# An mLSTM cell and a squared-ReLU feed-forward in one kernel: q C in twos, and another order of work in the first eight chunks

## The chip, the core and the metric

The kernel runs on one core of a Trainium2 chip. The metric is the device time of one execution in microseconds; the kernel before takes 527.05 us, the median of three runs (526.32 to 527.27). The core's engines are TensorE (PE in the profile, with its weight loads as PEld), VectorE (DVE), ScalarE (ACT), GpSimd (POOL) and the queues that start DMA transfers (SP). Each engine works through its own instructions in the order of the program and waits for the others by semaphores. The order within an engine is therefore part of the program, and a wait of one instruction holds up everything behind it on that engine.

## The reference, cut to what matters

Attention part: 4 batches, 8 heads, 768 steps, head size 40. A matrix memory C and a vector n are carried along the steps:

```python
for t in range(S):
    m_new  = np.maximum(f_gate[:, :, t] + m, i_gate[:, :, t])
    f_stab = np.exp(f_gate[:, :, t] + m - m_new)
    i_stab = np.exp(i_gate[:, :, t] - m_new)
    m = m_new
    C = f_stab * C + i_stab * outer(v_t, k_t)
    n = f_stab * n + i_stab * k_t
    h_tilde = C @ q_t
    denom = np.maximum(np.abs(n . q_t), 1.0)
    y[:, :, t] = sigmoid(o_gate_t) * h_tilde / denom
```

The result, taken as 3072 rows of 320 numbers, goes through the feed-forward part (w_in 320 x 2048, w_out 2048 x 320):

```python
h = np.maximum(x @ w_in, 0.0)
return h * h @ w_out
```

The weights arrive as 64-bit floats, that is as pairs of 32-bit words, and the kernel makes 32-bit floats of them itself ("rounding").

## The kernel before

The steps are cut into 24 chunks of 128. For each chunk TensorE turns k and q (chunks 0 to 6), forms the scores k q, and multiplies the weighted scores P with v, and, where the chunk is not the first of its batch, q with the memory C of the chunks before. VectorE weights the scores (`weighted`), normalises the result to x, squares the feed-forward's hidden values (`square_half`) and does most of the rounding. ScalarE makes the decay weights W, the relu and copies out of PSUM. Two chunks make a group of 256 rows for the feed-forward: `ffn1` (x w_in, in four steps a group) and `ffn2` (times w_out).

From chunk 6 on the attention works on turned tiles: q C and v P give num with the head's columns in the partitions. This is the kernel before, with P=128, H=8, PR=4, DP=64, D=40, D1=41:

```python
def attend_turned(s):
    ...
    halves = [slice(DP * i, DP * (i + 1)) for i in range(2)]
    live = [slice(DP * i, DP * i + D) for i in range(2)]
    numT = [ps_at.tile([P, W], F32, name="numT", tag="at")[:].rearrange("p (c t) -> p c t", t=P) for _ in range(2)]

    if c > 0:                                            # q C
        C = C_b[(s - 1) % 2]
        for e in range(2):
            for i, g in ((0, 0), (1, 1), (0, 1), (1, 0)):
                j = 2 * e + g
                nc.tensor.matmul(                        # L508
                    numT[i][halves[g], e, :], lhsT=C[live[i], j * D1 : j * D1 + DP], rhs=d["eA"][live[i], j, :],
                    start=(e == 0), stop=False, skip_group_check=True,
                )
    for i in range(2):                                   # v P
        for e in range(2):
            for g in range(2):
                ...
                nc.tensor.matmul(                        # L517
                    numT[i][halves[g], e, :], lhsT=va_w[s % NKQ][:, h * D1 : h * D1 + DP], rhs=..., ...)
    ...                                                  # dC (L527), then a DVE transpose of each numT (L534)
```

Rounding of one piece of the weights: two instructions on ScalarE (`words`), three on VectorE and an addition on GpSimd (`join`). A `step` does the words of the next piece ahead and joins one piece:

```python
def words(self):
    ...
    nc.scalar.activation(mag[:, :w], raw[:, :, 1].bitcast(F32), AF.Abs)                                   # L195
    nc.scalar.activation(low[:, :w], raw[:, :, 0].bitcast(U32), AF.Copy, bias=2.0, scale=2.0 ** -51)      # L197
def join(self):
    nc.vector.tensor_scalar(mag, mag, ...)                                     # L206
    nc.vector.tensor_scalar(bits, bits, scalar1=3, ..., op0=ALU.logical_shift_left)   # L210
    nc.vector.scalar_tensor_tensor(bits, in0=self.raws[n][:, :w, 1], ...)      # L211
    nc.gpsimd.tensor_tensor(dst.bitcast(I32), bits, low.bitcast(I32), op=ALU.add)     # L215
    self.fetch()
def step(self):
    if len(self.b) < len(pieces):
        if len(self.a) == len(self.b):
            self.words()
        self.words()
        self.join()
```

The start and the loop over chunks 2 to 5. `idle(n)` lets TensorE multiply n times with zeros; `weigh(s + 1)` masks on GpSimd (L358) and makes W on ScalarE (L382); P is made on VectorE (L433):

```python
idle(12)
transposes(0)                # four turns of k, then four of q, and their copies
idle(4)
scores(0)
idle(3)
...
for u in range(8):
    s = 2 + u // 2
    relu_half()                                  # ACT, L660
    if u % 2 == 0:
        if u == 0:
            ffn1(0, 0)
            scores(s)
            rounding.step()
        else:
            turn_rows(s - 1)                     # turns x on TensorE, L618
            scores(s)
            ffn1(u // 4, u % 4)
        ...
        weighted(s)
        if u == 2:
            ...
        else:
            weigh(s + 1)
            square_half()
    else:
        ...
        attend(s)                                # q C (L442), dC (L449), P v (L456)
        if u == 3:
            square_half()
        rounding.join()
        normalise(s)                             # L578 to L588, makes x
        ...
        transposes(s + 1)
        rounding.words()
        ffn1(u // 4, u % 4)
        square_half()
    ...
    while rounding.done < NEXT[u]:
        rounding.step()
```

ffn1 takes its PSUM tiles from a pool of three (`ps_h`) and uses two a step, so its second tile waits for a relu of the step before. The scores, dC, q C and num take theirs from another pool of three (`ps_at`).

The loop over the later parts; chunk s = 6 + n // 4. The pieces of weights end in its first five passes:

```python
LAST = (21, 23, 25, 25, 26)
for n, (which, g, i) in enumerate(parts):
    s, at = 6 + n // 4, n % 4
    ...
    if at == 0:
        do(score, s)                             # scores and weighted
    if at == 1:
        do(attend_turned, s)
        ...
    if which == 1:
        ...                                      # ffn1
            for half in both:
                st["half"] = half
                relu_half()
                square_half()
    elif g == 0:
        ffn2(g, *divmod(i, 2))
    else:
        ffn2_fast(g, i)
    ...
    if n < 5:
        while rounding.done < LAST[n]:
            rounding.step()
```

Of the kernel before, what the change touches and what calls it, by code (L numbers as in the profile page):

```python
# [29 lines left out]
def kernel(  # L30
# [85 lines left out]
    def make_consts():  # L116
        for t in kq_b:
            nc.vector.memset(t[:, :, :, D:], 0.0)
        for t in va_b:
            nc.vector.memset(t[:, :, D:], 1.0)  # L120
        for t in va_w:
            nc.gpsimd.memset(t[:, H * D1 :], 0.0)
        nc.vector.memset(keep[:], 1.0)
        nc.vector.memset(keep[:, :, 0:1], 0.0)
        make_identity(nc, ident[:])

        nc.gpsimd.memset(sel[:], 0.0)
        nc.gpsimd.affine_select(
            sel[:], sel[:], compare_op=ALU.not_equal, fill=1.0, base=0, pattern=[[-1, H], [0, P]], channel_multiplier=1,
        )  # L130

        nc.gpsimd.memset(later[:], 0.0)
        nc.gpsimd.affine_select(
            later[:], later[:], compare_op=ALU.is_ge, fill=-1e30, base=0, pattern=[[1, P]], channel_multiplier=-1,
        )

        nc.gpsimd.memset(bdm[:], 1.0)
        nc.gpsimd.memset(bdm[:DP, :, 1, :], 0.0)
        nc.gpsimd.memset(bdm[DP:, :, 0, :], 0.0)


    def in_words(ap):
# [20 lines left out]
    class Rounding:  # L163
# [56 lines left out]
        def done(self):  # L220
            return len(self.b)

        def step(self):
            if len(self.b) < len(pieces):
                if len(self.a) == len(self.b):
                    self.words()
                self.words()
                self.join()

    rounding = Rounding()  # L230
# [168 lines left out]
        t = ps_o.tile([P, W], F32, name="tp", tag="o_ps") if o else ps_at.tile([P, W], F32, name="tp", tag="at")  # L399
        return t[:].rearrange("p (j t) -> p j t", j=PR)  # L400

    def transposes(s, o=(False, False)):
        d = st[s]
        kqT(s)
        for i, n in enumerate(("kT", "qT")):
            tp = bank(o[i])
            for j in range(PR):
                nc.tensor.transpose(  # L408
                    tp[:, j, :], d["kq"][:, i, 2 * j : 2 * j + 2, :].rearrange("p h d -> p (h d)"), ident[:],
                )  # L410
            (nc.scalar.copy if i == 0 or s in (0, *range(2, 7)) else nc.vector.tensor_copy)(d[n], tp)
# [78 lines left out]

    def attend_turned(s):

        b, c = divmod(s, NB)
        d = st[s]
        halves = [slice(DP * i, DP * (i + 1)) for i in range(2)]
        live = [slice(DP * i, DP * i + D) for i in range(2)]  # L500
        numT = [ps_at.tile([P, W], F32, name="numT", tag="at")[:].rearrange("p (c t) -> p c t", t=P) for _ in range(2)]

        if c > 0:
            C = C_b[(s - 1) % 2]
            for e in range(2):
                for i, g in ((0, 0), (1, 1), (0, 1), (1, 0)):
                    j = 2 * e + g
                    nc.tensor.matmul(  # L508
                        numT[i][halves[g], e, :], lhsT=C[live[i], j * D1 : j * D1 + DP], rhs=d["eA"][live[i], j, :],
                        start=(e == 0), stop=False, skip_group_check=True,  # L510
                    )
        for i in range(2):
            for e in range(2):
                for g in range(2):
                    j = 2 * e + g
                    h = PR * i + j
                    nc.tensor.matmul(  # L517
                        numT[i][halves[g], e, :], lhsT=va_w[s % NKQ][:, h * D1 : h * D1 + DP],
                        rhs=d["P"][h % 2][:, h // 2, :] if s < KQ_SQ else d["P"][i][:, j, :],
                        start=(c == 0 and e == 0), stop=True, skip_group_check=True,  # L520
                    )
        if c + 1 < NB:
            dC = ps_at.tile([P, PR, D1], F32, name="dC", tag="at")
            for j in range(PR):
                for i in range(2):
                    h = PR * i + j
                    nc.tensor.matmul(  # L527
                        dC[live[i], j, :], lhsT=d["kq"][:, 0, h, :D], rhs=d["vw"][:, h, :], start=True, stop=True,
                    )

        tn = attn.tile([P, P // SQ, PR, SQ], F32, name="tn", bufs=1)
        to = tn[:].rearrange("p m c r -> p c m r")
        for i in range(2):
            nc.vector.transpose(to[:, 2 * i : 2 * i + 2], numT[i][:, :2, :].rearrange("p c t -> p (c t)"))  # L534
        d["tn"] = tn
        if c + 1 < NB:
            Cn = C_b[s % 2][:, : PR * D1].rearrange("p (j d) -> p j d", d=D1)
            for rows in live:
                if c > 0:
                    nc.vector.tensor_tensor(Cn[rows], dC[rows], d["Cd"][rows], op=ALU.add)  # L540
                else:
                    nc.vector.tensor_copy(Cn[rows], dC[rows])
# [13 lines left out]
    def normalise_turned(s):  # L556
        d = st[s]
        N = d["N"].rearrange("p (g e j r) -> p g e j r", g=2, e=2, r=SQ)
        R = D - SQ
        den = N[:, :, 1, :, R]  # L560
        dm = work.tile([P, H], F32, name="dm")
        dm2 = dm[:].rearrange("p (j g) -> p g j", g=2)
# [5 lines left out]
        x4, og = x[:, :DM].rearrange("p (j g d) -> p g j d", g=2, d=D), d["og"].rearrange("p (j g) d -> p g j d", g=2)  # L568
# [242 lines left out]
    load_part(1, 2)  # L811
    fetch(1)
    idle(12)
    transposes(0)
    idle(4)
    scores(0)
    idle(3)
# [49 lines left out]
            if u == 0:  # L867
                ffn1(0, 0)
                scores(s)
                rounding.step()  # L870
            else:
                turn_rows(s - 1)
                scores(s)
                ffn1(u // 4, u % 4)
            if u == 2:
                rounding.words()
            weighted(s)
            if u == 2:
# [31 lines left out]
        if u < 4:  # L910
            load_o(4 + u)
        while rounding.done < NEXT[u]:
            rounding.step()
# [23 lines left out]
    for n, (which, g, i) in enumerate(parts):  # L937
# [41 lines left out]
        if which == 1:  # L979
# [3 lines left out]
            else:  # L983
# [55 lines left out]
```

## Time and profile before

| | |
|---|---|
| time, median of 3 | 527.05 us (526.32 to 527.27) |
| span of the profiled execution | 525.2 us |
| mean granted clock of TensorE | 0.994 |
| L508, q C of the turned chunks | 240 records, 10.4 us busy |
| L517, v P of the turned chunks | 288 records, 19.7 us busy |
| L534, transposes of num on VectorE | 36, mean 447 ns |
| DMA | 68.06 MB, mean 130 GB/s |

The busy time in 40 equal slices of 13.1 us (a digit is tenths; the last three rows are not engines: granted clock of TensorE, busy share of the DMA engines):

```
PE   9989989998999999999999999999999999999997
PEld 4868878885798898898898898898898898998997
DVE  8588988968864764655754755665755755522541
ACT  3767577552541431522432623322623413102000
POOL 3355633231210210110210200110201210000000
PEclk9997999999999999999999999999999999999999
DMA  9989699777586586586586576676556262110000
```

The busy time of TensorE counts overlapping instructions once. The ends of matmuls are modelled, so how long a block of matmuls takes is better read from the start of its first instruction to the start of the next block. A line of the profile names the source line, the engine, the operation, what is written and read, the shape, the count, and in brackets the idle time before it with what ended it.

### The profile page before, as it was taken

What the parts mean: (1) busy time and instruction counts of PE and PEld (TensorE: products, weight loads), DVE (VectorE), ACT (ScalarE), POOL (GpSimd) and SP (SyncE); (2) the same over time, 40 slices, a digit from 0 to 9 for tenths busy, and PEclk for the clock granted to TensorE, in tenths of its full rate; (3) what the DMA queues carried; (4) which work ended last, traced back from release to release, by engine and by line L of the source; (5) the groups of instructions that cost most, each with busy time, mean ns of one, the idle gap of its engine ahead of it and who ended that gap; (6) DMA issues with size and microseconds to landing.
All of it is one profiled execution on the core that took longest, in us unless ns stands there. A gap on an engine that the chain in (4) does not pass through costs nothing.

```text
span 525.2 us, 10338 instructions
## 1 busy us (share of the span) xinstructions
PE 515.1 (98%) x3929; PEld 449.8 (86%) x3929; DVE 331.8 (63%) x638; ACT 194.2 (37%) x460; POOL 88.2 (17%) x110
## 2 busy tenths in 40 slices
PE   9989989998999999999999999999999999999997
PEld 4868878885798898898898898898898898998997
DVE  8588988968864764655754755665755755522541
ACT  3767577552541431522432623322623413102000
POOL 3355633231210210110210200110201210000000
PEclk9997999999999999999999999999999999999999
DMA  9989699777586586586586576676556262110000
GB/s 193 225 207 194 158 161 202 190 184 155 117 162 121 126 173 126 124 168 127 135 162 132 122 151 125 149 158 135 133 122 128 69 130 43 61 36 2 26 25 26
DMA packets 239394, 68.06 MB, mean 130 GB/s; under 512 B 185744, under 2 KB 233872, under 8 KB 239344
## 3 DMA queue, kind: packets, MB, share of 16 engines
q1 hardware_dynamic: 239248, 67.20, 60.5%
q8 instruction: 31, 0.51, 0.4%
q10 hardware_dynamic: 96, 0.20, 0.1%
q14 instruction: 19, 0.16, 0.1%
HBM read 55.08 MB, written 17.86 MB: 139 GB/s over the span
## 4 chain that ended last, share of the span: by engine, by line
PE 87%; DVE 5%; ACT 3%; DMA 2%; SPq 2%; issue 1%; POOL 0%; ACTq 0%; DVEq 0%; POOLq 0%
PE h_ps L728 33%; PE h_ps L634 27%; PE h_ps L645 7%; PE tp L420 4%; PE numT L517 3%; PE h_ps L674 2%; PE hp L456 2%; PE numT L508 2%; PE idle L787 1%; DVE g L667 1%; PE tp L408 1%; SPq L308 1%; DMA num_rows<-tn 1%; PE A_ps L349 1%; PE dC L527 1%
## 5 line engine op out<-in xcount | busy, mean ns | idle before, releaser
L634 PE MATMUL h_ps<-xT,w_in 128*128 128x256 f32 x768 | 175.7, 384 | 0.6 <-ACT xT L619 0.6
L634 PEld LDWEIGHTS h_ps<-xT,w_in 128*128 128x128 f32 x768 | 144.2, 191 | 22.0 <-issue 1.2
L667 DVE TENSOR_TENSOR g<-r_sb 128x512 f32<-128x512 f32 x96 | 61.7, 702 | 66.5 <-ACT r_sb L660 66.5
L660 ACT ACTIVATE r_sb<-h_ps 128x512 f32<-128x512 f32 x96 | 49.9, 600 | 108.6 <-PE h_ps L645 105.5
L728 PE MATMUL h_ps<-w_out,g 128*128 128x160 f32 x528 | 77.0, 302 | 0.0
L728 PEld LDWEIGHTS h_ps<-w_out,g 128*128 128x128 f32 x528 | 72.5, 190 | 1.4
L358 POOL TENSOR_SCALAR_AFFINE_SELECT A_bc<-A_bc 128x1024 f32<-128x1024 f32 x22 | 24.3, 1103 | 214.2 <-ACT kq L368 155.4
L382 ACT ACTIVATE W_sb<-A_bc,b_T 128x128 f32<-128x128 f32 x176 | 53.8, 390 | 13.3 <-POOL A_bc L358 13.1
L728 PE MATMUL h_ps<-T,S 128*128 128x160 f32 x352 | 52.3, 302 | 0.0
L728 PEld LDWEIGHTS h_ps<-T,S 128*128 128x128 f32 x352 | 48.8, 190 | 3.0 <-ACT r_sb L660 3.0
L368 ACT ACTIVATE kq<-A_bc 64x512 f32<-64x512 f32 x30 | 18.9, 629 | 84.3 <-DMA A_bc<-a_rows 84.2
L645 PE MATMUL h_ps<-xT,w_in 64*128 64x256 f32 x384 | 49.0, 391 | 0.0
L645 PEld LDWEIGHTS h_ps<-xT,w_in 64*128 64x128 f32 x384 | 34.8, 186 | 12.3 <-issue 9.0
L744 DVE TENSOR_TENSOR y_sb<-y_sb,h_ps 128x160 f32<-128x160 f32 x44 | 14.1, 320 | 29.3 <-PE h_ps L728 28.7
L433 DVE TENSOR_TENSOR P_sb<-tp,W_sb 128x512 f32<-128x512 f32 x46 | 29.5, 684 | 3.6 <-PE tp L420 3.1
L534 DVE STREAM_TRANSPOSE tn<-numT 128x256 f32<-128x256 f32 x36 | 15.7, 447 | 23.2 <-PE numT L517 23.2
L394 POOL TENSOR_TENSOR vw<-va,W_sb 128x328 f32<-128x328 f32 x20 | 18.1, 904 | 66.0 <-ACT W_sb L382 60.3
L748 ACT COPY y_sb<-h_ps 128x160 f32<-128x160 f32 x11 | 3.2, 293 | 66.3 <-PE h_ps L728 66.3
L420 PEld LDWEIGHTS tp<-kqT 40*128 40x128 f32 x384 | 24.2, 187 | 3.3 <-issue 2.3
L420 PE MATMUL tp<-kqT 40*128 40x128 f32 x384 | 26.9, 279 | 0.0
L728 PE MATMUL h_ps<-T,g 128*128 128x160 f32 x176 | 25.7, 299 | 0.0
L728 PE MATMUL h_ps<-w_out,S 128*128 128x160 f32 x176 | 25.7, 299 | 0.0
(119 smaller groups left out, 592.0 us busy)
## 6 DMA issues: line engine op xcount, KB each, us to landing
A_bc<-a_rows SPq DMA_DIRECT2D x23, 512.0 KB, 4.7
raw<-in_moe_w_out_dram SPq DMA_DIRECT2D x16, 320.0 KB, 3.5
num_rows<-tn SPq DMA_DIRECT2D x18, 256.0 KB, 3.1
kq<-num_rows SPq DMA_DIRECT2D x72, 64.0 KB, 2.2
kqT<-kq_rows SPq DMA_DIRECT2D x34, 128.0 KB, 3.2
raw<-in_moe_w_in_dram SPq DMA_DIRECT2D x8, 512.0 KB, 5.2
kq<-in_k_dram SPq DMA_DIRECT2D x24, 160.0 KB, 4.7
va<-in_v_dram SPq DMA_DIRECT2D x24, 160.0 KB, 4.9
```

The lines of the kernel that those rows point to most:

```text
L358: nc.gpsimd.affine_select(A[:], A[:], compare_op=ALU.is_ge, fill=-1e30, base=0, pattern=[[0, H], [1, P]], channel_multiplier=-1,)
L368: nc.scalar.activation(e[rows], st[s]["A"][0][rows, PR * i : PR * (i + 1), :], AF.Exp)
L382: nc.scalar.activation(d["W"][:, i * n + h, :], A[i][:, h, :], AF.Exp, bias=b_T[:, b, c, i * n + h : i * n + h + 1],)
L394: nc.gpsimd.tensor_tensor(d["vw"][:], d["va"][:], d["W"][:, :, P - 1 : P].to_broadcast([P, H, D1]), op=ALU.mult,)
L420: nc.tensor.matmul(sc[i][:, j, :], lhsT=d["kT"][rows, j, :], rhs=d["qT"][rows, j, :], start=True, stop=True,)
L433: nc.vector.tensor_tensor(t, d["sc"][i], d["W"][:, heads, :], op=ALU.mult)
L517: nc.tensor.matmul(numT[i][halves[g], e, :], lhsT=va_w[s % NKQ][:, h * D1 : h * D1 + DP], rhs=d["P"][h % 2][:, h // 2, :] if s < KQ_SQ els ...
L634: nc.tensor.matmul(hs[i][:, n, :], lhsT=w_in[:, a, fb * P : (fb + 1) * P], rhs=xT[:, :, a, :], start=(n == 0 and a == 0), stop=False,)
L645: nc.tensor.matmul(hs[i][:, n, :], lhsT=w_in2[rows, 2 * pp + n, :], rhs=xT[rows, :, 2, :], start=False, stop=(n == 1),)
L660: nc.scalar.activation(rs[-1][:], h[:], AF.Relu)
L667: nc.vector.tensor_tensor(g4[:, :, i, :], r[:], r[:], op=ALU.mult)
L728: nc.tensor.matmul(to, lhsT=lhsT[:, p], rhs=rhs[:, p, :], start=(start and p == 0), stop=(p == NPAIR - 1), skip_group_check=True,)
```

## The change

The kernel after differs in these places.

- q C of the turned chunks: one num tile in one PSUM bank in place of two; pairs of matmuls (rows 0 to 39 of C into partitions 0 to 63, rows 64 to 103 into partitions 64 to 127) in place of groups of four over all row and column halves. v P follows the same order, one VectorE transpose takes the place of two, and normalisation reads the heads in the new order.
- First chunk: four multiplications with zeros between the turns of k and those of q, so that TensorE goes on working there. The zeroing of the ends of the v tiles on GpSimd comes later among the constants.
- Chunk 2: P is made ahead of the rounding step, so that TensorE need not wait for it behind that.
- Chunk 3: normalisation comes ahead of a rounding.
- Last pieces of weights: the words of the last piece are no longer made ahead, and the squares of pass 3 come after chunk 7's P in pass 4, so that P waits neither for the last transfer of weights nor for the squares.

```diff
-        for t in va_w:
-            nc.gpsimd.memset(t[:, H * D1 :], 0.0)
 ...
+        for t in va_w:
+            nc.gpsimd.memset(t[:, H * D1 :], 0.0)
 ...
-        def step(self):
+        def step(self, ahead=True):
             if len(self.b) < len(pieces):
                 if len(self.a) == len(self.b):
                     self.words()
-                self.words()
+                if ahead:
+                    self.words()
                 self.join()
 ...
-    def transposes(s, o=(False, False)):
+    def transposes(s, o=(False, False), apart=0):
 ...
         for i, n in enumerate(("kT", "qT")):
+            if i > 0 and apart:
+                idle(apart)
             tp = bank(o[i])
 ...
-        numT = [ps_at.tile([P, W], F32, name="numT", tag="at")[:].rearrange("p (c t) -> p c t", t=P) for _ in range(2)]
+        numT = ps_at.tile([P, PR, P], F32, name="numT", tag="at")
 ...
-            for e in range(2):
-                for i, g in ((0, 0), (1, 1), (0, 1), (1, 0)):
-                    j = 2 * e + g
+            for j in range(PR):
+                for i in range(2):
                     nc.tensor.matmul(
-                        numT[i][halves[g], e, :], lhsT=C[live[i], j * D1 : j * D1 + DP], rhs=d["eA"][live[i], j, :],
-                        start=(e == 0), stop=False, skip_group_check=True,
+                        numT[halves[i], j, :], lhsT=C[live[i], j * D1 : j * D1 + DP], rhs=d["eA"][live[i], j, :],
+                        start=(j == 0), stop=False, skip_group_check=True,
                     )
 ...  (v P in the same order)
-        for i in range(2):
-            nc.vector.transpose(to[:, 2 * i : 2 * i + 2], numT[i][:, :2, :].rearrange("p c t -> p (c t)"))
+        nc.vector.transpose(tn[:].rearrange("p m j r -> p j m r"), numT[:].rearrange("p j t -> p (j t)"))
 ...  (the order of heads in normalise_turned)
-    transposes(0)
+    transposes(0, apart=4)
 ...
             if u == 0:
                 ffn1(0, 0)
                 scores(s)
+                weighted(s)
                 rounding.step()
 ...
-            weighted(s)
+            if u > 0:
+                weighted(s)
 ...
             if u == 3:
                 square_half()
-            rounding.join()
-            normalise(s)
+                normalise(s)
+                rounding.join()
+            else:
+                rounding.join()
+                normalise(s)
 ...
         if at == 0:
             do(score, s)
+            if n == 4:
+                square_half()
+                square_half()
 ...
                     relu_half()
-                    square_half()
+                    if n != 3:
+                        square_half()
 ...
-                rounding.step()
+                rounding.step(ahead=rounding.done + 1 < LAST[2])
```

More of the change, by code (lines that the diff above doesn't have):

```diff
@@ L500, in attend_turned @@
         live = [slice(DP * i, DP * i + D) for i in range(2)]
-        numT = [ps_at.tile([P, W], F32, name="numT", tag="at")[:].rearrange("p (c t) -> p c t", t=P) for _ in range(2)]
+        numT = ps_at.tile([P, PR, P], F32, name="numT", tag="at")
         if c > 0:
             C = C_b[(s - 1) % 2]
-            for e in range(2):
-                for i, g in ((0, 0), (1, 1), (0, 1), (1, 0)):
-                    j = 2 * e + g
+            for j in range(PR):
+                for i in range(2):
                     nc.tensor.matmul(
-                        numT[i][halves[g], e, :], lhsT=C[live[i], j * D1 : j * D1 + DP], rhs=d["eA"][live[i], j, :],
-                        start=(e == 0), stop=False, skip_group_check=True,
-                    )
-        for i in range(2):
[L513 to L521, printed above, removed]
+                        numT[halves[i], j, :], lhsT=C[live[i], j * D1 : j * D1 + DP], rhs=d["eA"][live[i], j, :],
+                        start=(j == 0), stop=False, skip_group_check=True,
+                    )
+        for j in range(PR):
+            for i in range(2):
+                h = PR * i + j
+                nc.tensor.matmul(
+                    numT[halves[i], j, :], lhsT=va_w[s % NKQ][:, h * D1 : h * D1 + DP],
+                    rhs=d["P"][h % 2][:, h // 2, :] if s < KQ_SQ else d["P"][i][:, j, :],
+                    start=(c == 0 and j == 0), stop=True, skip_group_check=True,
+                )
         if c + 1 < NB:
@@ L531, in attend_turned @@
         tn = attn.tile([P, P // SQ, PR, SQ], F32, name="tn", bufs=1)
-        to = tn[:].rearrange("p m c r -> p c m r")
-        for i in range(2):
-            nc.vector.transpose(to[:, 2 * i : 2 * i + 2], numT[i][:, :2, :].rearrange("p c t -> p (c t)"))
+        nc.vector.transpose(tn[:].rearrange("p m j r -> p j m r"), numT[:].rearrange("p j t -> p (j t)"))
         d["tn"] = tn
@@ L561, in normalise_turned @@
         dm = work.tile([P, H], F32, name="dm")
-        dm2 = dm[:].rearrange("p (j g) -> p g j", g=2)
+        dm2 = dm[:].rearrange("p (g j) -> p g j", g=2)
         nc.vector.tensor_scalar(dm2, den, scalar1=-1.0, scalar2=1.0, op0=ALU.mult, op1=ALU.max)
@@ L567, in normalise_turned @@
         x3 = x[:, :DM].rearrange("p (h d) -> p h d", d=D)
-        x4, og = x[:, :DM].rearrange("p (j g d) -> p g j d", g=2, d=D), d["og"].rearrange("p (j g) d -> p g j d", g=2)
+        x4, og = x[:, :DM].rearrange("p (g j d) -> p g j d", g=2, d=D), d["og"].rearrange("p (g j) d -> p g j d", g=2)
         nc.vector.tensor_tensor(x4[:, :, :, :SQ], N[:, :, 0], og[:, :, :, :SQ], op=ALU.mult)
```

## The prediction

> **What bounds the kernel now.** I read the busy times first, then the list of waits of TensorE, then the single instructions of the stages that the diff touches.
>
> ```profile
> PE 515.1 (98%) x3929; PEld 449.8 (86%) x3929; DVE 331.8 (63%) x638; ACT 194.2 (37%) x460; POOL 88.2 (17%) x110
> ```
> TensorE (PE) is busy for 515.1 of 525.2 us. So the end moves for two reasons only: TensorE work is added or removed, or one of its few waits goes. Those waits, by what was waited for (total, times, longest):
>
> ```profile
> PE numT L508 <- DVE P_sb L433: 2.6, 1, 2.6
> PE tp L618 <- DVE x_sb L587: 1.7, 1, 1.7
> PE dC L449 <- DVE P_sb L433: 1.1, 1, 1.1
> PE h_ps L634 <- ACT xT L619: 0.6, 1, 0.6
> ```
> By start time they lie at 127.7, 68.2, 39.5 and 31.7 us; from 128 us to the end TensorE has no gap. Three are the targets of the diff: the last words and squares (127.7), chunk 3's normalisation (68.2), P of chunk 2 (39.5). After the last one, stretches of the span (length, then busy time and count for PE, PE loads, DVE, ACT, POOL, then TensorE's granted clock) show a second loss:
>
> ```profile
> 37.50:40.95 3.45, 2.37 (x22) 2.25 (x21) 3.08 (x6) 0.25 (x1) 2.29 (x3) 1.00 0.68 151
> 40.95:44.40 3.45, 3.45 (x19) 3.45 (x19) 2.54 (x6) 3.17 (x11) 0.89 (x2) 0.50 1.04 283
> 44.40:47.80 3.40, 3.40 (x11) 2.86 (x11) 3.30 (x5) 3.35 (x7) 3.16 (x4) 0.51 1.42 159
> ```
> Clock 0.50 for 6.8 us right after the wait: some 3.4 us of TensorE time.
>
> The part that the change undoes stands in each turned chunk. TensorE in order of time (start, length):
>
> ```profile
> 148.39 0.67 PE L508 MATMUL numT<-kq,C 40*64 40x128 f32 x16
> 148.99 1.09 PE L517 MATMUL numT<-P_sb,va 128*64 128x128 f32 x16
> 149.91 0.48 PE L527 MATMUL dC<-vw,kq 128*40 128x41 f32 x16
> ```
> q C (L508) and v P (L517) each have 16 records, two for each of 8 matmuls with 128 columns, but from start to start q C takes 0.60 us and v P 0.92. The single records show why: q C starts in fours, at 148.55, 148.66, 148.77 (109 ns apart); v P in twos, also 109 ns apart.
>
> [...] four q C records within 20 ns, and 172 ns without a weight load before q C and before v P. [...] The new q C pairs take different rows and different halves of one bank, [...] only v P's pairs (one bank, two halves, 109 ns) come near that, no trace has exactly the new form. [...] The trace shows the halving after 1.08 us of idling among small matmuls, but none after 1.75 and 2.6 us, [...]. [...] the shift L210 takes 0.43 us alone and 1.40 beside GpSimd.
>
> **The change part by part.**
>
> 1. q C in twos. Eight matmuls of two records: 4 groups of four x 109 ns = 436 ns become 8 pairs x 109 = 872 ns. [...] L508 has 240 records, 240 / 16 = 15 chunks. TensorE has no slack after 128 us, so all of it counts: 15 x 0.436 = **+6.5 us**. One VectorE transpose of 512 columns in place of two of 256 (0.45 us each), one PSUM bank less, and another order of heads: all off the path.
>
> 2. Last words and squares. ScalarE and VectorE around the wait of 127.7:
>
> ```profile
> 123.04 0.50 ACT L195 ACTIVATE mag<-raw 128x320 f32<-128x320 f32 x1 [5.75 <-DMA raw<-in_moe_w_out_dram]
> 123.84 2.04 ACT L660 ACTIVATE r_sb<-h_ps 128x512 f32<-128x512 f32 x4
> 124.44 2.50 DVE L667 TENSOR_TENSOR g<-r_sb 128x512 f32<-128x512 f32 x4 [1.64 <-ACT r_sb L660]
> 126.97 1.29 DVE L433 TENSOR_TENSOR P_sb<-tp,W_sb 128x512 f32<-128x512 f32 x2
> ```
> The last weight words wait for a DMA, the relus stand behind the words, the squares behind the relus, chunk 7's P behind the squares. Afterwards P comes right after the rounding at 122.8 and ends near 124.1; the q C of chunk 7 starts near 124.7 less the 1.2 gained earlier (below) and takes about 1.0, so v P, the first to need P, is due near 124.5. The q C of chunk 7 lasts from 124.69 to 128.38 = 3.69 us instead of 0.60: **-3.1 us**. The last rounded piece of w_out then lands near 128.6; the product needs it only near 130, so no new wait.
>
> 3. Chunk 3's normalisation. VectorE ends the wait of 68.2, and has no gap from 43.5 to 68.2:
>
> ```profile
> 62.59 0.85 DVE L206 TENSOR_SCALAR mag<-mag 128x320 f32<-128x320 f32 x1
> ...
> 64.84 0.49 DVE L578 TENSOR_TENSOR num<-num,hp 128x328 f32<-128x328 f32 x1
> ...
> 67.58 0.49 DVE L587 TENSOR_TENSOR x_sb<-x_sb,dm 128x320 f32<-128x320 f32 x1
> ```
> The rounding from 62.59 to 64.84 (2.25 us) moves behind. x is then ready at 68.1 - 2.25 = 65.8, before TensorE is free at 66.46: the gap of 1.75 goes, and not more unless TensorE itself is earlier. **Up to -1.75 us.**
>
> 4. Zeros between the first k and q turns. Four matmuls of 0.214 us = 0.86 us in front of everything. TensorE has no gap from 1 to 27.5 us, and the scan that makes A ends at 10.1, just as TensorE reaches the spreading of A (10.00), so nothing takes the shift up: **+0.8 us** at 27.5.
>
> 5. P of chunk 2 ahead of a rounding. The scores end at 37.4 + 0.86 = 38.3; P's first half is ready at 39.05, dC starts at 39.2: no gap, and by this the clock should hold. But VectorE pays: it now idles from 35.5 to 38.4 where it had a rounding to do, and that rounding ends at 41.2 instead of 38.7. Behind it stand GpSimd's addition (1.3) and the mask of chunk 3 (1.1, before until 41.2, now 43.7), then W (2.4), then the relu whose PSUM buffer the next ffn1 needs. That relu moves from 43.7 to 46.3; ffn1's second half starts near 46.9 (before about 47.5, at half clock). I follow VectorE on: addition and next rounding, normalisation of chunk 2 from 44.55 (before 43.53) but with less GpSimd beside it, P of chunk 3 at 53.6 (before 53.33). So VectorE is about 0.3 us late when step 3 begins: shift and saved contention nearly cancel, and the 3.4 us of half clock bring nothing at the end, because VectorE was the bound there.
>
> At chunk 3's x: VectorE 68.1 + 0.3 - 2.25 = 66.1; TensorE, tied to the rounded pieces by the same 0.3, is free at 66.7; before 68.2. So steps 3 to 5 together give -1.5 us; TensorE's new hole near 44.5 to 46.9 may halve the clock once more, which I put at a mean of +0.3: **-1.2 us**.
>
> Sum: 527.05 + 6.5 - 3.1 - 1.2 = 529.25, say **529.2 us**.
>
> **The rivals.** (a) The early part gives more: all waits of 1.1, 1.75 and 3.1 and the half clock of 3.4 count in full: -9.3 + 6.5 + 0.8, about 525. For it: the half clock is real. Against it: no gap on VectorE between 43.5 and 68.2. (b) The new hole in TensorE halves the clock for 6.8 us and the early part gives nothing: 527.05 + 6.5 - 3.1 + 0.5 = 531. For it: a wait of 1.1 us was enough before. Against it: 1.75 and 2.6 were not. (c) Two row tiles in one bank don't overlap: each q C then takes 16 x 0.109 = 1.74 us, 15 x 1.3 = +19.6 us, about 542. [...] (d) q C in twos is hidden: it would need a TensorE wait after 128 us to absorb it, and there is none.
>
> **Range and chances.** The 6.5 is counted from steady records and good to 0.3; the 3.1 to 0.5; the early part lies between -3.5 and +1. That gives 526.8 to 531.6. The 2% limits are 516.5 and 537.6: the upper is reached only by (c), the lower by nothing I see. Faster 0.01, same 0.965, slower 0.025.
>
> **What would show it.** Right: q C at about 1.03 us from start to start in 15 chunks, records in twos 109 ns apart; no wait at chunk 7's q C; chunk 3's x before TensorE asks; A matmuls starting near 10.9; the relu of the first ffn1 near 46; the stretch of half clock from 41 to 47.8 gone. Wrong: q C above 1.5 us a chunk (c), clock 0.5 between 47 and 58 (b), chunk 3's turn of x before 65.5 (a), or a new TensorE wait after 128 us.

## The result, and the profile after

The changed kernel takes 528.82 us, the median of four runs (528.50 to 529.65), against 527.16 us of the kernel before in four runs beside it. The ratio is 1.0037, with a 95% interval of 1.0020 to 1.0054. The prediction of 529.2 us holds: the kernel is a little slower. The span of the profiled execution grew from 525.2 to 526.9 us.

First the busy times and the row of the granted clock in 40 slices (here 13.2 us each) of the kernel after:

```profile
PE 519.8 (99%) x3933; PEld 453.8 (86%) x3933; DVE 328.6 (62%) x620; ACT 193.9 (37%) x460; POOL 91.5 (17%) x110
PEclk9998999999999999999999999999999999999999
```

TensorE is busy for 4.7 us more and the span is 1.7 us longer: idle time was taken out, and more work put in. What is left of TensorE's waits (what waited, for what, total us, times, longest):

```profile
PE h_ps L628 <- ACT r_sb L654: 2.3, 1, 2.3
PE idle L781 <- DVE zeros L776: 0.9, 1, 0.9
PE h_ps L628 <- ACT xT L613: 0.6, 1, 0.6
```

The waits for P of chunk 2, for x of chunk 3 and for P of chunk 7 are gone. One new wait stands on top, of the first feed-forward step for a relu.

The added work is in the turned chunks. TensorE in order of time, chunks 7 and 8 (start, length):

```profile
123.02 1.09 PE L506 MATMUL numT<-kq,C 40*64 40x128 f32 x16
124.04 1.09 PE L513 MATMUL numT<-P_sb,va 128*64 128x128 f32 x16
...
144.12 1.09 PE L506 MATMUL numT<-kq,C 40*64 40x128 f32 x16
145.15 1.09 PE L513 MATMUL numT<-P_sb,va 128*64 128x128 f32 x16
```

q C (L506) now takes 1.02 us from its start to the start of v P, where it took 0.60; chunk 8's first records start at 144.284, 144.393 and 144.502, in twos 109 ns apart. Chunk 7 shows no wait between q C and v P. ScalarE and VectorE show why:

```profile
120.50 0.50 ACT L195 ACTIVATE mag<-raw 128x320 f32<-128x320 f32 x1 [1.52 <-DMA raw<-in_moe_w_out_dram]
```
```profile
120.88 1.29 DVE L436 TENSOR_TENSOR P_sb<-tp,W_sb 128x512 f32<-128x512 f32 x2
122.09 2.49 DVE L661 TENSOR_TENSOR g<-r_sb 128x512 f32<-128x512 f32 x4
```

P of chunk 7 (L436) follows the rounding before it (till 120.85) directly, and the squares (L661) come behind it. P is done at 122.2, before q C even starts.

In the kernel before, q C of chunk 7 stood waiting after its first two records:

```profile
124.69 0.43 PE L508 MATMUL numT<-kq,C 40*64 40x128 f32 x2
127.72 0.66 PE L508 MATMUL numT<-kq,C 40*64 40x128 f32 x14 [2.60 <-DVE P_sb L433]
128.31 1.09 PE L517 MATMUL numT<-P_sb,va 128*64 128x128 f32 x16
```

In chunk 3, VectorE and TensorE of the kernel after, and then TensorE of the kernel before:

```profile
65.20 0.49 DVE L581 TENSOR_TENSOR x_sb<-x_sb,dm 128x320 f32<-128x320 f32 x1
...
65.84 0.32 DVE L206 TENSOR_SCALAR mag<-mag 128x320 f32<-128x320 f32 x1
```
```profile
66.43 0.55 PE L612 MATMUL tp<-ident,x_sb 128*128 128x128 f32 x3
```
```profile
68.21 0.52 PE L618 MATMUL tp<-ident,x_sb 128*128 128x128 f32 x3 [1.75 <-DVE x_sb L587]
```

x is ready by the time the rounding (L206) begins, 65.84, ahead of TensorE, which turns it at 66.43 and not at 68.21.

So the difference of the two spans can be told at three places. q C of chunk 7 starts 1.67 us earlier (124.69 to 123.02). Its v P starts 4.27 us earlier (128.31 to 124.04), which is 1.67 and 2.60 of a vanished wait. The last v P starts 1.65 us later (445.005 to 446.657): 14 chunks with 0.423 us more each gave back 5.92.

What took the place of the early half clock is seen in the stretches of 37.5 to 51.2 us (length, then busy time and count of PE, PE loads, DVE, ACT, POOL, then granted clock, DMA share, GB/s):

```profile
37.50:40.95 3.45, 3.45 (x32) 3.44 (x33) 3.33 (x7) 0.32 (x1) 0.48 (x2) 1.00 0.38 75
40.95:44.40 3.45, 2.91 (x19) 2.35 (x18) 3.38 (x5) 1.36 (x5) 2.06 (x2) 1.00 0.84 225
44.40:47.80 3.40, 1.67 (x4) 1.40 (x5) 3.23 (x9) 3.40 (x10) 2.23 (x2) 0.73 1.20 222
47.80:51.20 3.40, 3.40 (x18) 2.13 (x17) 3.33 (x4) 2.63 (x6) 2.62 (x3) 0.77 1.18 240
```

The half clock of 40.9 to 47.8 is gone. In its place TensorE has a hole and a shorter half clock: the clock records show 0.5 from 45.98 to 49.40. VectorE is busy throughout. The hole's chain, engine by engine:

```profile
41.97 1.89 PE L628 MATMUL h_ps<-xT,w_in 128*128 128x256 f32 x8
46.13 3.59 PE L628 MATMUL h_ps<-xT,w_in 128*128 128x256 f32 x8 [2.27 <-ACT r_sb L654]
```
```profile
37.55 1.29 DVE L436 TENSOR_TENSOR P_sb<-tp,W_sb 128x512 f32<-128x512 f32 x2 [2.74 <-PE tp L423]
```
```profile
40.50 1.27 POOL L215 TENSOR_TENSOR w_in<-mag,low 128x512 int32<-128x512 int32 x1 [2.97 <-DVE mag L211]
41.73 1.28 POOL L359 TENSOR_SCALAR_AFFINE_SELECT A_bc<-A_bc 128x1024 f32<-128x1024 f32 x1
```
```profile
43.04 2.45 ACT L383 ACTIVATE W_sb<-A_bc,b_T 128x128 f32<-128x128 f32 x8 [5.22 <-POOL A_bc L359]
45.50 1.06 ACT L654 ACTIVATE r_sb<-h_ps 128x512 f32<-128x512 f32 x2
```

VectorE waits 2.74 us for the scores before it makes P, the rounding behind it is late, and GpSimd's addition, the mask, W and the relu follow in a row. TensorE waits 2.27 us for that relu.

### The profile page after: what moved, and what is told of

Read it like the earlier page. It is cut to its first block, busy times and chain, and to the rows that moved or that the text cites. A ratio compares the mean times of both kernels' runs of the same rounds, so it can differ in the third digit from the quotient of the medians.

```text
span 526.9 us, 10341 instructions
## 1 busy us (share of the span) xinstructions
PE 519.8 (99%) x3933; PEld 453.8 (86%) x3933; DVE 328.6 (62%) x620; ACT 193.9 (37%) x460; POOL 91.5 (17%) x110
## 4 chain that ended last, share of the span: by engine, by line
PE 96%; DVE 3%; DMA 1%; issue 0%; POOL 0%; ACT 0%; DVEq 0%; SPq 0%; POOLq 0%
PE h_ps L722 33%; PE h_ps L628 32%; PE h_ps L639 9%; PE tp L423 4%; PE numT L513 4%; PE h_ps L668 3%; PE numT L506 3%; PE hp L459 2%; PE idle L781 1%; PE tp L411 1%; PE dC L523 1%; PE A_ps L350 1%; PE hi L445 1%; PE A_ps L346 1%; PE dC L452 1%; DMA raw<-in_moe_w_in_dram 1%
## 5 line engine op out<-in xcount | busy, mean ns | idle before, releaser
L661 DVE TENSOR_TENSOR g<-r_sb 128x512 f32<-128x512 f32 x96 | 62.9, 714 | 67.1 <-ACT r_sb L654 67.1
L359 POOL TENSOR_SCALAR_AFFINE_SELECT A_bc<-A_bc 128x1024 f32<-128x1024 f32 x22 | 26.2, 1190 | 213.0 <-ACT kq L369 141.0
L528 DVE STREAM_TRANSPOSE tn<-numT 128x512 f32<-128x512 f32 x18 | 12.9, 717 | 36.1 <-PE numT L513 36.1
L436 DVE TENSOR_TENSOR P_sb<-tp,W_sb 128x512 f32<-128x512 f32 x46 | 29.5, 684 | 4.9 <-PE tp L423 4.3
```

The source lines that it names most:

```text
L359: nc.gpsimd.affine_select(A[:], A[:], compare_op=ALU.is_ge, fill=-1e30, base=0, pattern=[[0, H], [1, P]], channel_multiplier=-1,)
L436: nc.vector.tensor_tensor(t, d["sc"][i], d["W"][:, heads, :], op=ALU.mult)
L661: nc.vector.tensor_tensor(g4[:, :, i, :], r[:], r[:], op=ALU.mult)
```

## The experiments

The kernels ran in three groups; each group had its own runs of the kernel before beside it: median 529.53 us in 11 runs (group 1), 527.88 in 46 (group 2), 528.15 in 27 (group 3). Within a group medians can be compared. Across groups the ratios are given too, though the scatter of the kernel before is in them. Most experiments start from one kernel, called "fours": the kernel after, with q C as it was before. Its line numbers are up to 9 higher than the kernel after's (relu L663, turn of x L621, squares L670).

**q C in fours, all else as after** (group 1). Edit to the kernel after:

```diff
-            for j in range(PR):
-                for i in range(2):
+            for e in range(2):
+                for i, g in ((0, 0), (1, 1), (0, 1), (1, 0)):
+                    j = 2 * e + g
 ...   (numT of two banks, v P, transposes and order of heads as before, too)
```

> The new order of the first eight chunks with q C left in fours. My theory (the parts add up): the early part gives 1.7 us at chunk 6's v P and 3.0 us at chunk 7's q C, q C stays at 0.60 us in all 15 chunks, so 527.1 - 4.7 = 522.4 us (521.8 to 523.0). Rival: chunk 7's q C escaped its wait only because the pairs need one PSUM bank and not two; then a wait of 2 us or more comes back at chunk 7's q C and the time is 524.4 us or more.

Measured: 522.82 us (522.53 to 523.21, 6 runs), ratio 0.9886 (0.9864 to 0.9908). This part of the change alone turns a faster kernel into a slower one. The profile has no half clock at all after the start, but a wait that the kernel after doesn't have. TensorE:

```profile
46.49 1.99 PE L637 MATMUL h_ps<-xT,w_in 128*128 128x256 f32 x8 [2.27 <-ACT r_sb L663]
...
53.40 3.29 PE L637 MATMUL h_ps<-xT,w_in 128*128 128x256 f32 x14 [1.65 <-POOL w_in L215]
...
66.80 0.55 PE L621 MATMUL tp<-ident,x_sb 128*128 128x128 f32 x3
```

The same hole of 2.27 us, this time at full clock; TensorE then arrives earlier and waits 1.65 us for a rounded piece of w_in. x of chunk 3 is turned at 66.80, no earlier than in the kernel after (66.43) with its half clock. From the start of chunk 2's P to this turn it is 28.89 us here (from 37.91) and 28.88 in the kernel after (from 37.55). So the half clock at 46 to 49 cost nothing there, as step 5 of the prediction had it for the one at 41 to 48.

**q C in twos, all else as before** (group 2): the reverse edit on the kernel before.

> The kernel before with nothing but q C, v P, the transposes of num and the normalisation in the new form (one bank, twos). My theory: 0.423 us in each of 15 chunks, that of chunk 7 hidden in its wait, so 5.9 to 6.4 us more than the kernel before beside it (ratio 1.011 to 1.012), 533 us if that is at 527. Rival (hidden behind other engines): less than 3 us more.

Measured: 533.72 us (532.74 to 534.56, 6 runs), ratio 1.0104 (1.0085 to 1.0124), 5.8 us over the runs beside it, just under the expected 5.9 to 6.4. Of the 15 times 0.42 us, 14 count (5.9) and one is hidden, in the wait for P of chunk 7:

```profile
124.67 1.09 PE L503 MATMUL numT<-kq,C 40*64 40x128 f32 x16
127.51 0.43 PE L510 MATMUL numT<-P_sb,va 128*64 128x128 f32 x2 [1.75 <-DVE P_sb L433]
```

q C, which takes one bank of its pool here and no longer two, runs through, and the wait stands at v P.

**Both kernels again** (group 2), without an edit.

> The changed kernel itself once more, because the kernel before ran between 526.8 and 530.9 us beside the last runs and no longer between 526.3 and 527.4. Theory (the half clock falls on other places in each execution of the kernel before, and the new order of the first chunks takes that scatter away): the changed kernel keeps 529.2 us within 0.7 and a spread of about 1 us, the kernel before spreads by 3 us or more. Rival (all kernels are slower on that chip): the changed kernel is at 531.5 us with the ratio of 1.0037 kept.

> The kernel before once more, for where its half clock lies. Theory: 6.8 us of half clock after the wait for chunk 2's P again, and in an execution above 529 us a further stretch of it elsewhere in the first 70 us. Rival: the same stretch of half clock as before at any time, and the difference lies after 130 us.

Measured: after 529.05 us (528.20 to 530.02, 22 runs), ratio 1.0019 (1.0005 to 1.0032); before 528.10 us (526.12 to 531.62, 20 runs), ratio 0.9991 (0.9975 to 1.0007). The kernel before scatters over 5.5 us here, the kernel after over 1.8 (about 1 was expected), and the rival for the kernel after, a slower chip with the ratio kept, does not hold. The profile of this run of before has the three waits, somewhat longer, and half clock after two of them (41.17 to 48.00 and 129.92 to 133.33):

```profile
PE tp L618 <- DVE x_sb L587: 3.0, 2, 1.8
PE numT L508 <- DVE P_sb L433: 3.0, 1, 3.0
PE dC L449 <- DVE P_sb L433: 1.1, 1, 1.1
```

The half clock after chunk 2's P was expected. The further stretch was expected in the first 70 us and lies at 129.92, so that part of the theory is wrong and the rival is nearer. In the profile that the prediction had read, the clock was not halved after the wait for P of chunk 7. The mean granted clock of each run tells how often it happens; a stretch of 3.41 us at half clock lowers it by 0.0032 (the kernel after, with one, has 0.9968). The 84 runs of the kernel before that stood beside the experiments, and all 26 of the kernel after:

| mean granted clock | before: runs, median us | after: runs, median us |
|---|---|---|
| 0.999 to 1.000 | 2, 525.0 | 6, 528.6 |
| 0.997 | 9, 527.5 | 19, 529.2 |
| 0.993 to 0.994 | 27, 527.3 | 1, 530.0 |
| 0.990 | 30, 529.0 | none |
| 0.987 or less | 16, 529.6 | none |

The 20 runs of before without an edit lie alike (527.5, 526.7, 528.8 and 528.9 us from the second row down). So most runs of before lose two to four such stretches (two profiles show where, after the waits), and on the whole their time rises by about 1 us for each (4.6 us between the first row and the last); the kernel after loses one at most in 25 of 26.

**The old last words and squares** (group 2), on "fours":

```diff
-            if n == 4:
-                square_half()
-                square_half()
 ...
-                    if n != 3:
-                        square_half()
+                    square_half()
 ...
-                rounding.step(ahead=rounding.done + 1 < LAST[2])
+                rounding.step()
```

> As the run with fours, but the last words ahead and the squares of pass 3 ahead of chunk 7's P again. My theory: the wait of 2.6 us or more comes back at chunk 7's q C and nothing else changes, 522.8 + 3.0 = 525.8 us. Rival (the last transfer of weights lands in time once TensorE is earlier or later, so no wait): 522.8 us.

Measured: 524.78 us (523.97 to 527.79, 9 runs), ratio 0.9946 (0.9926 to 0.9965); 2.0 us over "fours" by the medians and some 3 by the ratios; in the profiles v P of chunk 7 starts 2.09 us later (126.08 and 123.99). The wait comes back, shorter than in the kernel before:

```profile
123.53 0.43 PE L511 MATMUL numT<-kq,C 40*64 40x128 f32 x2
125.48 0.66 PE L511 MATMUL numT<-kq,C 40*64 40x128 f32 x14 [1.53 <-DVE P_sb L436]
```

The squares start at 121.76 here and at 124.44 in the profile of before, 2.7 us earlier, while TensorE is only 1.2 earlier. With the early part mended, the wait that step 2 removes is 1.5 us in this profile and not 2.6: the two parts overlap.

**Chunk 3's normalisation behind the rounding again** (group 3), on "fours":

```diff
-                normalise(s)
-                rounding.join()
-            else:
-                rounding.join()
-                normalise(s)
+            rounding.join()
+            normalise(s)
```

> The kernel with q C in fours and all the other parts of the change, but with chunk 3's normalisation behind the rounding step again, as it stood before. Theory: the turn of chunk 3's x comes about 1.7 us later (near 68.2 us instead of 66.8), TensorE waits there for VectorE, and the whole is about 1.5 us longer than with the normalisation ahead: 524.3 us. Rival: the wait only moves (TensorE is late at that place anyway), and the time stays at 522.8 within 0.4.

Measured: 526.49 us (525.75 to 528.07, 22 runs), ratio 0.9973 (0.9960 to 0.9987). That is 3.7 us above "fours" by the medians, and more by the ratios: both expectations were too small. VectorE and TensorE:

```profile
64.53 0.85 DVE L206 TENSOR_SCALAR mag<-mag 128x320 f32<-128x320 f32 x1
...
68.73 1.26 DVE L590 TENSOR_TENSOR x_sb<-x_sb,dm 128x320 f32<-128x320 f32 x1
```
```profile
70.14 0.52 PE L621 MATMUL tp<-ident,x_sb 128*128 128x128 f32 x3 [2.28 <-DVE x_sb L590]
```

The turn of x is 3.34 us later than in "fours" (70.14 against 66.80). About 1.0 of it was there before the edited place is reached: a half clock from 14.50 to 17.92 let P of chunk 2 start at 38.91 and not at 37.91. The other 2.3 are the order itself. The rounding of 2.25 us (from 64.53) stands ahead, and x is finished later still, because its last product takes 1.26 us beside the mask on GpSimd (68.25 to 69.65) where it took 0.49. All 22 runs show a mean clock of 0.992 to 0.994, so two stretches of half clock, and none of "fours" shows more than one. As the early one lies ahead of the edit, whether the order causes the second stretch in every run stays open.

**P of chunk 2 behind the rounding again** (group 1), on "fours":

```diff
-                weighted(s)
                 rounding.step()
 ...
-            if u > 0:
-                weighted(s)
+            weighted(s)
```

> As the run with fours, but P of chunk 2 behind the rounding step again. Theory of the prediction (VectorE sets the end of this stretch, so P of chunk 2 first brings nothing): 522.4 us within 0.6, although a TensorE wait of 1.1 us near 39.5 and 6.8 us of half clock come back; the turn of chunk 3's x starts near 66.5 us as with P first. Rival (waits and half clock count in full): 4 us slower than with P first, 526 us or more.

Measured: 523.11 us (521.41 to 524.97, 6 runs), ratio 0.9887 (0.9857 to 0.9916). The median is 0.3 us from "fours", well inside its own scatter. That is near the theory and far from the rival. The wait for P is back, and in the profile half clock from 14.83 to 18.24 and from 42.13 to 48.96:

```profile
41.07 1.09 PE L452 MATMUL dC<-vw,kq 128*128 128x82 f32 x8 [1.06 <-DVE P_sb L436]
```

P of chunk 2 starts 2.33 us later than in "fours" (40.24), the turn of chunk 3's x only 1.17 later (67.97), and in the run above an early half clock alone had delayed P by 1.0. The runs come in pairs: 521.6 us at a mean clock of 1.000, 523.1 at 0.993, 524.4 at 0.990. By these pairs, P ahead costs about 1.2 us where the clock would not have been halved, and saves 0.3 to 1.6 where it would. At the median it brings nothing, and it makes the time steady: "fours" stayed within 0.7 us.

**No zeros between the turns** (group 1), on "fours":

```diff
-    transposes(0, apart=4)
+    transposes(0)
```

> As the run with fours, without the four zero matmuls between the first k and q turns. Theory of the prediction (they cost their own 0.86 us): 521.5 us, and the A matmuls start 0.8 us earlier than with them (near 9.2 if the clock rises at 5.0 us, near 10.0 if it rises at 6.8). Rival (the clock's rise, which falls elsewhere from run to run, decides): same time as with the zeros within 0.4 us, about 522.4 us. A second rival, that the zeros keep the clock up: without them TensorE has half clock again before 10 us and the time is above 523 us.

Measured: 522.30 us (521.87 to 523.08, 6 runs), ratio 0.9878 (0.9855 to 0.9900), 0.5 us under "fours" with overlapping ranges. That is nearer to the rival (within 0.4) than to the theory (0.9 less). In its profile the spreading of A starts at 9.65, in that of "fours" at 9.61, but the clock rose at different moments. The starts of the kernel after, for comparison:

```profile
0.93 4.77 PE L781 MATMUL idle<-zeros 128*128 128x512 bf16 x12 [0.93 <-DVE zeros L776]
...
5.97 1.03 PE L781 MATMUL idle<-zeros 128*128 128x512 bf16 x4
...
10.00 1.02 PE L346 MATMUL A_ps<-later,ident 128*128 128x512 f32 x2
```

The first twelve products run at half clock until the clock rises (in the kernel after they start 427 ns apart up to 4.75 us and 217 to 220 from 5.10 on), and that moment differs from run to run: 3.84 us in "fours", 5.02 in this profile of the kernel after, 6.08 without the zeros, 6.81 in the first profile of before, 3.62 in its second. After a late rise the added zeros cost their full time. A with them, in the run with the old last words (rise at 5.86), and without them (rise at 6.08):

```profile
10.41 1.02 PE L346 MATMUL A_ps<-later,ident 128*128 128x512 f32 x2
```
```profile
9.65 1.02 PE L346 MATMUL A_ps<-later,ident 128*128 128x512 f32 x2
```

These are 0.76 us apart, and 0.87 when half of the 0.22 us between the rises is added. After an early rise TensorE would have waited for q in their place (0.69 us at 6.21 in the second profile of before).

**W of chunk 3 ahead of the rounding step** (group 1), on "fours", an attempt to close the new hole:

```diff
                 weighted(s)
+                weigh(s + 1)
                 rounding.step()
 ...
-                weigh(s + 1)
+                if u > 0:
+                    weigh(s + 1)
```

> As the run with fours, with chunk 3's mask and W ahead of the rounding step too, which should remove the wait of 2.3 us of TensorE for the first relu near 44 us and the half clock behind it. My theory: TensorE then meets the next rounded piece of w_in (ready near 52.5 us) instead, so the turn of chunk 3's x comes only 0.3 us earlier: 522.1 us. Rival (the hole counts in full): 520.1 us or less, no new wait.

Measured: 524.72 us (522.44 to 525.35, 6 runs), ratio 0.9913 (0.9887 to 0.9940): slower than "fours" by 1.9, which neither theory had. The hole at 46 is gone. W on ScalarE now stands ahead of the next words, and VectorE waits for these, but the piece of w_in does not come later for it: TensorE has it at 53.01, in "fours" at 53.40. VectorE and TensorE:

```profile
42.06 1.55 DVE L206 TENSOR_SCALAR mag<-mag 128x512 f32<-128x512 f32 x1 [0.67 <-ACT mag L195]
```
```profile
53.01 4.91 PE L637 MATMUL h_ps<-xT,w_in 128*128 128x256 f32 x14 [2.07 <-POOL w_in L215]
...
375.17 2.03 PE L731 MATMUL h_ps<-w_out,S 128*128 128x160 f32 x13 [1.15 <-DVE y_sb L747]
```

The time is lost behind that wait. The clock is halved from 52.92 to 56.34, so that 14 products take 4.91 us and not 3.29, and x of chunk 3 is turned at 68.03, 1.23 later than in "fours". About as much again is lost with the wait at 375 us, which no other profile has; why it came, and whether the other runs have it, stays open. The profiled run is the slowest of the six. The one at a mean clock of 1.000 took 522.44 us, near the theory's 522.1.

**The mask alone ahead** (group 3), and **the same without the zeros** (group 3). The edit to "fours":

```diff
                 weighted(s)
+                mask(s + 1)
                 rounding.step()
 ...
-                weigh(s + 1)
+                weigh(s + 1, masked=(u == 0))
```

> The kernel with q C in fours and all the other parts, in which the mask of chunk 3 (GpSimd) alone is issued ahead of the rounding step and W of chunk 3 stays behind it. Theory: GpSimd no longer waits for VectorE, W of chunk 3 and the first relu come about 3 us earlier (relu near 42 us), TensorE's hole of 2.3 us at 46 goes, VectorE is not delayed, and TensorE then waits 1 to 2 us for a rounded piece of w_in: about 521.0 us. Rival one: new waits take all of it, 522.8 or more. Rival two: the hole's 2.3 us come off in full, 520.5.

> The same with the mask ahead, without the zero products between the first k and q turns. Theory: the zeros cost 0.1 to 0.85 us by when the clock rises, so about 0.5 us less than with them: 520.5 us. Rival: the zeros keep the clock up later, and without them a half clock comes back near 47 us: 522 or more.

Measured: 522.34 us (521.91 to 522.99, 6 runs), ratio 0.9888 (0.9865 to 0.9912), and 522.43 us (521.00 to 522.71, 6 runs), ratio 0.9884 (0.9859 to 0.9908). By the time, nothing clear is gained over "fours" (522.82 us, 0.9886), and nothing by the second over the first. TensorE with the mask ahead, and then without the zeros too:

```profile
48.80 0.52 PE L621 MATMUL tp<-ident,x_sb 128*128 128x128 f32 x3 [0.71 <-ACT low L197]
...
53.11 3.29 PE L637 MATMUL h_ps<-xT,w_in 128*128 128x256 f32 x14 [2.07 <-POOL w_in L215]
...
66.51 0.55 PE L621 MATMUL tp<-ident,x_sb 128*128 128x128 f32 x3
```
```profile
51.69 4.97 PE L637 MATMUL h_ps<-xT,w_in 128*128 128x256 f32 x14 [2.08 <-POOL w_in L215]
```

The hole closes in both, and on the engines something is gained. From the start of chunk 2's P to the products that wait for the piece of w_in it is 14.13 us (38.98 to 53.11) and 14.14 (37.55 to 51.69), in "fours" 15.49 (37.91 to 53.40). Half clock took this back. In the first profile it fell at 14.59, and P of chunk 2 itself started 1.07 us later than in "fours". In the second it fell at 51.96, right behind the wait for w_in and not near 47, where the rival had it, and the 14 products take 4.97 us in place of 3.29.

At full clock the turn of chunk 3's x follows the piece of w_in by 13.40 us ("fours" 53.40 to 66.80, the mask ahead 53.11 to 66.51), in the second profile by 15.09. So this piece, the end of a chain of roundings on VectorE, sets the pace of the stretch: half clock ahead of it was covered, half clock behind it counted. The one run of each at a mean clock of 1.000 took 521.91 and 521.00 us, that of "fours" 522.83. One run each does not show what the mask ahead brings at full clock.

## Why the prediction was right

**Step 1, q C in twos (+6.5).** Right: 0.423 us a chunk against 0.436, 15 chunks give 6.35. The times without a weight load before q C and before v P stayed (171 and 172 ns in chunk 8; 172 for both in the kernel before). "Fours" against the kernel after shows it alone: 522.82 and 529.05 us, 6.2 us (some 7 by the ratios, good to about 1.3). That the pairs would run two at a time was the author's estimate from v P's pairs (one bank, two halves, 109 ns apart in the kernel before). Rival (c) is refuted: the pairs of q C, which write two halves of one bank, run 109 ns apart, the two of a pair 7 ns apart. Rival (d) is refuted as well: in twos alone the time grew by 5.8.

**Step 2, last words and squares (-3.1).** Right in the pair of profiles: from the start of q C to the start of v P chunk 7 took 3.62 us and now takes 1.02, which is 2.60 less with the 0.42 of step 1 in it, so 3.0 for this part. (The prediction's 3.69 ran to the modelled end of q C and not to the start of v P.) Undone alone it measured only 2.0, since the wait is 1.5 once the early part is mended.

**Step 3, chunk 3's order (up to -1.75).** Right in where it acts: x was ready at 65.8 (predicted 66.1), TensorE free at 66.43 (66.7). The size was that of the old kernel's gap. In the new order the same edit is worth 2.3 us of the turn by one profile, and 3.7 us by the medians of "fours" with and without it; the difference is partly half clock elsewhere, as said above.

**Step 4, zeros (+0.8).** The cost was right, what the step left out is that the clock's rise moves. The spreading of A was expected at 10.9 and started at 10.00, as before. But the clock rose at 5.02 in this profile and at 6.81 in the one that was read, and 1.79 us more at full clock are worth 0.9 us of TensorE's work, just what the four products cost. With late rises the cost shows (10.41 against 9.65, above). Over many runs the zeros cost 0.5 us at one pair of medians and nothing at the other, whose half clock lay elsewhere.

**Step 5, P of chunk 2 first.** The chain was right, link by link: a rounding late by the wait for the scores, the mask, W, the relu at 45.5 (46.3), the hole from 43.9 to 46.1 (44.5 to 46.9), P of chunk 3 at 53.91 (53.6), and nothing at the end, because VectorE is the bound there. That the times fit so well is partly luck: P of chunk 2 started at 37.55 and not at 38.4, as the early rise of the clock would have it (step 4), and from there to P of chunk 3 VectorE took 16.36 us and not 15.2. Undone alone it moves the median by 0.3. Rival (b)'s half clock did come, for 3.4 us and not 6.8, and cost nothing, since w_in would have been waited for anyway. Rival (a) was wrong about the median. It had a point that the prediction missed: other runs of the kernel before lose more half clock than the profiled one, as its second profile does after the wait for P of chunk 7, which had looked harmless.

The sum: without step 1 the prediction had -4.3 us. "Fours" is 5.3 us under the second set of runs of before by medians, and by its ratio of 0.9886 some 6.0, with an interval of 1.2 to each side. So steps 2 to 5 were put too low by about 1 us in the mean of many runs, and step 1 too high by 0.2. Undone alone they come to 2.0 us (step 2), 3.7 (3), 0.3 (5) and -0.5 (4), 5.5 together: step 2 was put too high by 1.1, and steps 3 to 5, of which 1.2 was expected, too low by 2.3, the half clock of step 3's run in it. The later zeroing of the v tiles was not undone alone.

The mechanism was right, but that the time was met within 0.4 us is partly luck. The three runs behind the 527.05 lay about 1 us under the later median of before (528.10), and the gain was put too low by about as much. The difference between the two kernels was predicted as 2.2 us and came out as 1.7 in the first comparison and 1.0 over many runs (ratio 1.0019). The range held.

## What to carry to other kernels

Where one engine is busy to the end, a packing that halves its rate in a small, frequent step is worth counting record by record: 0.42 us in 15 chunks undid all that the removal of three waits had brought, and the kernel with these waits removed and q C still in fours is faster than both. Closing a hole of the busiest engine pays only if the next thing it needs is there; look for the next wait behind the hole before moving anything. Half clock ahead of such a wait was covered here (28.88 us from chunk 2's P to the turn of chunk 3's x with it, 28.89 without), half clock behind it was not (14 products in 4.97 us and not 3.29). One profile shows one position of the clock's grid (below; its first rise came between 3.62 and 6.81 us), so judge edits that only remove short waits by many runs, and by their scatter as well as by the median.

## What the runs showed of the hardware that was not expected

- Whether half clock followed a wait went with where the wait lay. The clock's later falls and rises come whole steps of 3.413 us after the first rise: in the kernel after the fall 12 steps (5.02 to 45.98) and the rise 13, in the first profile of before 10 and 12 (6.81 to 40.94 and 47.77), in the second the falls 11 and 37 (3.62 to 41.17 and 129.92). The hole of 2.27 us had 2.12 of it in one stretch of this grid in the kernel after, and the next stretch ran at half clock; in "fours" a border cut it into 0.58 and 1.69, and the clock stayed. The wait for P of chunk 7 was cut into 1.16 and 1.45 in the first profile of before (no fall) and into 0.77 and 2.22 in the second (fall). Half clock also followed the stretches with 2.0 us of the wait for w_in in the run with W first and 2.08 in that with the mask ahead and no zeros. It did not follow those with 1.10 of it with the mask ahead and 1.65 in "fours", nor the 1.75 of the wait for x in the first profile of before.
- Idle time is not the whole of it. The wait for P of chunk 2, among products of 41 to 82 columns, left 1.06 to 1.08 us in one stretch in the first profile of before and in the run with this P behind the rounding, and 6.8 us of half clock followed (40.94 to 47.77, 42.13 to 48.96). In three of the experiments' profiles the clock also fell near 14.5 us (14.50, 14.59, 14.83). In the first of them, that of chunk 3's old order, TensorE shows no wait from 9.64 us to the fall and multiplies small tiles of 32 x 32 just before it (L261, 13.72 to 14.60).
- The clock's first rise came anywhere from 3.62 us (second profile of before) to 6.81 us (first) into the span, with the same twelve products ahead of it.
- An elementwise product of 128 x 320 on VectorE took 0.49 us alone (at 65.20 in the kernel after) and 1.26 beside a mask on GpSimd (at 68.73 in the run with chunk 3's old order).
